# Second product of the expert network in 512 columns with two results added, later first counts, and pass A behind the first placement

## The chip, the cores and the metric

The kernel runs on one core of a Trainium2 chip. The metric is device time in microseconds (us) of one execution; the median of three runs of the kernel before is 1425.91 us.

## The reference

A Fourier filter along the sequence feeds a mixture of experts with eight experts, each with room for an eighth of the 19968 tokens:

```python
X = np.fft.rfft(x, axis=1)                      # x: 8 x 2496 x 256
y = np.fft.irfft(X * (filt_r + 1j * filt_i)[None], n=2496, axis=1)
tok = y.reshape(19968, 256)
logits = tok @ w_gate                           # 8 experts
# greedy: all (token, expert) pairs by falling logit; a pair is taken if the
# token is still free and the expert has fewer than 2496 tokens
for e in range(8):
    h = np.maximum(tok[mask_e] @ w1[e], 0.0)    # 256 -> 1024
    out[mask_e] = h @ w2[e]                     # 1024 -> 256
```

## The kernel before

The kernel has two stages that overlap a little: the Fourier filter as matmuls (class `Fft`, up to some 400 us), and the experts (class `Ffn`) one after the other. Routing (class `Route`) is done in eight phases. A phase finds the next expert to be full, with its members; it runs beside the network of the expert before it.

**The expert network.** An expert's 2496 tokens are five groups g: four of 512 and one of 448. A group's tokens are gathered, turned (L844) and split into a high and a low part of fp32r, whose sum is the fp32 value. `first` does the first product: for each of eight slices f of the hidden size, six matmuls of 512 columns into a PSUM tile `pz` (L864), then ScalarE's Relu writes the high part of the result and VectorE the low part, both in `hl` (L891, L893; in the last group L896, in two pieces). The second product runs over blocks t of 128 tokens (four in a group, the last one of the fifth group a half block of 64): in each step f, the stationary operand is a 128 x 128 piece of `hl` and the moving one 256 columns of the second weight. Three terms are summed: high times high (`w2h`), high times low (`w2l`), low times high, each one matmul of 256 columns into the PSUM tile `py` (L930). `py` has two buffers of tag "b". After 24 matmuls ScalarE copies `py` to `y` (L940) and a scatter on the GpSimd queue writes the rows out (L941). The half block puts high and low parts side by side as 128 columns of weights, in 16 matmuls, and adds the two halves of its result (L937, L938). The trace shows names of the first weight's tiles for some of the second's: `py<-w1h` in its rows is the product with `w2h`, and `pz<-xo,w0h` that with `w1h`.

**Weights.** `split` makes high and low tiles of the next expert's weights out of the loaded ones, eight parts of 512 columns an expert, ScalarE the high part and VectorE the low one (L823, L824).

**Routing beside it.** A phase from the second on begins with passes over the logits on VectorE: the maximum M (L644), two passes over `tmp` (L646, L648), the reduction to `ar` (L650), and pass A (L654), which marks for each token its best free expert. Eleven rounds of counts follow (`counts`): a comparison pass Gm on VectorE (L559), then eleven or thirteen short matmuls over Gm and A into a PSUM tile `rt` of tag "a" (two buffers; L567), three small VectorE passes (L575 to L577), and one matmul (L580) whose result sets the next threshold. The first count of a phase has three thresholds (nj = 3), the later ones seven or nine. When a phase has its members, `places` turns them to lists of rows for the gathers and the scatters, in five chunks, each with matmuls into `rt` (L777), VectorE passes (L778, L782) and ScalarE passes (L781). `s.last` is the VectorE instruction that ends the list of the first chunk (L787, L789).

**What sets the order.** TensorE's instructions are issued in the order in which the code is written. `Pump` sets where the routing's instructions go among the network's matmuls: each `yield` of the network gives the planner the time of the matmuls just issued, and each step of the routing gives a kind and a size, from which `lag` makes the time that must pass until the next step is issued. For a count, 'G' stands between the comparison pass and its matmuls, 'X' between the small passes and the matmul of L580. `ORD` says how many first products of the next group stand ahead of each block: one, none, none, one. The other engines' order is made by the framework's scheduler out of its own timeline; `issue_after` keeps an instruction behind another in it.

Of the kernel before, what the change touches and what calls it, by code (L numbers as in the profile page):

```python
# [7 lines left out]
F32, F32R = mybir.dt.float32, mybir.dt.float32r  # L8
# [7 lines left out]
G = 22  # L16
S = B * G
# [449 lines left out]
class Route:  # L467
# [169 lines left out]
    def phase(s, ph):  # L637
# [4 lines left out]
        if 0 < ph < 7:  # L642
            with s.tc.issue_after(s.last):
                nc.vector.tensor_reduce(s.M, s.lg, axis=AX.X, op=OP.max)  # L644
            yield 'd', 5.5
            nc.vector.tensor_tensor(s.tmp, s.lg, s.M.unsqueeze(2).to_broadcast([117, S, 8]), op=OP.is_equal)  # L646
            yield 'd', 1.5
            nc.vector.tensor_tensor(s.tmp, s.tmp, s.val[:117].unsqueeze(1).to_broadcast([117, S, 8]), op=OP.mult)  # L648
            yield 'd', 1.5
            nc.vector.tensor_reduce(s.ar, s.tmp, axis=AX.X, op=OP.max)  # L650
            nc.vector.scalar_tensor_tensor(s.ar, s.asg, 0.0, s.ar, op0=OP.is_equal, op1=OP.mult)
            yield 'd', 1.8
            n = s.n = 8 - ph
            nc.vector.tensor_tensor(s.A[:, :S*n].rearrange("p (s e) -> p s e", e=n), s.ar.unsqueeze(2).to_broadcast([117, S, n]),  # L654
                                    s.desc[:117, :n].unsqueeze(1).to_broadcast([117, S, n]), op=OP.is_equal)
            s.room()
            yield 'd', 1.5
        if ph < 7:
# [139 lines left out]
class Ffn:  # L798
# [9 lines left out]
    def weights(s, e, widx):  # L808
        nc = s.nc
        raw = [s.ww.tile([128, 2048], F32, name=f"wr{k}", bufs=1) for k in range(2)]  # L810
        off = bass.IndirectOffsetOnAxis(ap=widx[:, :1], axis=0)
        hl = [[s.ww.tile([128, 2048], F32R, name=f"w{k}{h}", bufs=2) for h in 'hl'] for k in range(2)]
        s.wt[e] = (raw, hl)
        s.load = lambda k: nc.gpsimd.indirect_dma_start(out=raw[k], out_offset=None, in_=(s.w1, s.w2)[k], in_offset=off).ins

    def split(s, e, part):

        nc = s.nc
        raw, hl = s.wt[e]
        k, h = divmod(part, 4)  # L820
        o = 512 * (h if k else 2 * (h % 2) + h // 2)
        src, hi, lo = (t[:, o:o+512] for t in (raw[k], *hl[k]))
        nc.scalar.copy(hi, src)  # L823
        nc.vector.tensor_tensor(lo, src, hi.bitcast(F32), op=OP.subtract)  # L824

# [24 lines left out]
    def run(s, e, pump, hook):  # L850
# [1 line left out]
        nc = s.nc  # L852
        ids = pump.out[e]
        out_rows = s.out
        _, ((w1h, w1l), (w2h, w2l)) = s.wt[e]
        hs = {}

        def products(p, f, g, a, b):
# [53 lines left out]
        for g in range(5):  # L912
            n = min(512, CAP - 512*g)
            yield from firsts(g, 8)
            if g == 4:
                hook('last')
            if g == 0:
                hook('w2')
            for t in range(4):
                if g < 4:  # L920
                    yield from firsts(g + 1, ORD[t])
                w = min(128, n - 128*t)
                p = s.ps.tile([128, D], F32, name="py", tag="b", bufs=2)
                half = w == 64
                hi, lo, both = slice(128*t, 128*t+w), slice(512+128*t, 512+128*t+w), slice(384, 512)
                terms = ((both, w2h), (hi, w2l)) if half else ((hi, w2h), (hi, w2l), (lo, w2h))
                m = 0
                for f in range(8):
                    for a, b in terms:
                        nc.tensor.matmul(p[:a.stop-a.start], hs[g][f][:, a], b[:, 256*f:256*f+256],  # L930
                                         start=m == 0, stop=m == 8 * len(terms) - 1, skip_group_check=half)
                        m += 1
                    if f in ((3,) if half else (1, 3, 5)):
                        yield 0.65
                y = s.wp.tile([128, D], F32, name="y", bufs=4)
                if half:
                    nc.scalar.copy(y[:w], p[w:])  # L937
                    nc.vector.tensor_tensor(y[:w], p[:w], y[:w], op=OP.add)  # L938
                else:
                    s.lasta = nc.scalar.copy(y, p).ins  # L940
                st = nc.gpsimd.indirect_dma_start(  # L941
                    out=out_rows, out_offset=bass.IndirectOffsetOnAxis(ap=ids[1][:w, 4*g+t:4*g+t+1], axis=0),
                    in_=y[:w], in_offset=None)
                for o in s.scat:
                    s.tc.declare_no_dep(st.ins, o.ins, reason="each token has one place")
                s.scat.append(st)
                if t in (1, 2) and g == 4:
                    hook(t)
                yield 0.65
# [147 lines left out]
class Pump:  # L1097
# [3 lines left out]
    def __init__(s, R):  # L1101
# [1 line left out]
        s.main, s.due, s.held = R.phase(0), 0.0, False  # L1103
        s.side = []
        s.on_w, s.kind = None, ''
        s.lag = dict(d=lambda t: t, G=lambda n: LAGS[s.ph][0] + 0.17 * n, X=lambda n: LAGS[s.ph][1], m=lambda t: 1.0 + 1.2*t, w=lambda t: t,
                     o=lambda t: t, p=lambda t: t, g=lambda t: 3.0)

    def step_main(s):
        if s.held:  # L1110
# [71 lines left out]
```

## Time and profile before

| | before |
|---|---|
| median of three runs | 1425.91 us (1425.71 to 1428.44) |
| the profiled execution | 1423.78 us, span 1422.0 us |
| TensorE matmul / weight loads | 97% / 86% of the span |
| VectorE / ScalarE / GpSimd | 63% / 47% / 35% |
| instructions of TensorE | 10412 matmuls, as many weight loads |
| mean granted clock of TensorE | 0.991 of full speed |

The rows are read so: "out<-in" are the program's names of the tiles, then partitions x elements, then how many; "idle before" is the time an engine stood before these instructions, and behind the arrow stands what ended it. Ends of matmuls are modelled, so that the pace of TensorE is read from one start to the next. A line of a stretch gives its start and end, its length, and the busy time of TensorE's matmuls, its weight loads, VectorE, ScalarE and GpSimd in it, with the number of instructions.

### The profile page before, as it was taken

How to read it: one execution, taken by the hardware profiler on the slowest of the kernel's cores; microseconds unless marked ns; L12 is line 12 of the kernel's file. 1: busy time of each engine (PE TensorE's matmuls, PEld its weight loads, DVE VectorE, ACT ScalarE, POOL GpSimd, SP SyncE). 2: the span in 40 equal slices, each digit the busy share in tenths (PEclk: the TensorE clock that was granted, in tenths of full speed). 3: DMA queues.
4: the chain of work that ended last, by engine and by line, in shares of the span. 5: the costliest groups of instructions: out<-in, count | busy, mean ns of one | idle time of the engine just before them, and what ended most of it. 6: DMA issues, size and time to landing. Idle time of an engine off the chain costs nothing.

```text
span 1422.0 us, 27350 instructions
## 1 busy us (share of the span) xinstructions
PE 1385.4 (97%) x10412; PEld 1216.9 (86%) x10412; DVE 893.8 (63%) x2554; ACT 672.0 (47%) x1632; POOL 503.6 (35%) x562
## 2 busy tenths in 40 slices
PE   9999999999989999999999999999999999999997
PEld 8998898976467898988789889888898998898987
DVE  5577676775667777568667876866867634423231
ACT  6766676645544254236335534523623635423231
POOL 3344343443034135324322733343334324333312
PEclk9999999999989999999999999999999999999999
DMA  9665664539961022112112212112111311111100
GB/s 375 250 228 182 197 217 132 165 106 297 367 224 58 16 97 66 36 53 78 50 33 83 67 43 89 46 48 99 46 44 50 136 52 55 47 39 50 40 19 28
DMA packets 57846, 153.12 MB, mean 108 GB/s; under 512 B 11023, under 2 KB 31519, under 8 KB 54131
## 3 DMA queue, kind: packets, MB, share of 16 engines
q0 software_dynamic: 22720, 72.67, 15.6%
q1 hardware_dynamic: 29132, 73.39, 14.9%
q10 hardware_dynamic: 5863, 5.31, 1.1%
q8 instruction: 82, 1.34, 0.4%
q14 instruction: 49, 0.40, 0.1%
HBM read 88.32 MB, written 63.06 MB: 106 GB/s over the span
## 4 chain that ended last, share of the span: by engine, by line
PE 42%; issue 6%; DVE 4%; POOL 1%; ACT 1%; DMA 0%; POOLq 0%; ACTq 0%; another core or an unknown queue 0%; DVEq 0%
PE py L930 20%; PE pz L864 19%; PE ptr L844 2%; POOL out L941 1%; PE rt L567 1%; PE rt L777 1%; DVE hl L896 1%; DVE w1l L824 0%; DVE hl L893 0%; DVE M L644 0%; DVE tmp L646 0%; ACT junka L781 0%; DVE tmp L648 0%; ACT hl L891 0%; DVE Gm L559 0%
## 5 line engine op out<-in xcount | busy, mean ns | idle before, releaser
L930 PE MATMUL py<-w1h,hl 128*128 128x256 f32 x2496 | 481.6, 286 | 0.8 <-DVE hl L896 0.8
L930 PEld LDWEIGHTS py<-w1h,hl 128*128 128x128 f32 x2496 | 400.9, 191 | 3.6 <-DVE hl L896 1.2
L930 PE MATMUL py<-w1l,hl 128*128 128x256 f32 (+1 forms) x1280 | 358.1, 282 | 0.0
L941 POOL DMA_INDIRECT out<-y,oid x160 | 169.2, 1058 | 501.1 <-ACT y L940 452.6
L891 ACT ACTIVATE hl<-pz 128x512 fp32r<-128x512 f32 (+1 forms) x320 | 187.7, 588 | 229.4 <-PE pz L864 186.6
L864 PE MATMUL pz<-xo,w0h 128*128 128x512 f32 (+2 forms) x646 | 265.8, 411 | 2.7 <-DVE hl L893 1.2
L893 DVE SCALAR_TENSOR_TENSOR hl<-pz,hl 128x512 fp32r<-128x512 f32 x256 | 175.4, 687 | 139.3 <-ACT hl L891 136.5
L864 PE MATMUL pz<-xo,w0l 128*128 128x512 f32 (+2 forms) x646 | 251.5, 389 | 0.0
L864 PE MATMUL pz<-z,w0h 128*128 128x512 f32 (+2 forms) x646 | 251.1, 389 | 0.3
L930 PEld LDWEIGHTS py<-w1l,hl 128*128 128x128 f32 (+1 forms) x1280 | 239.8, 187 | 2.1
L830 POOL DMA_INDIRECT xg<-xs,xid x160 | 172.4, 1077 | 145.9 <-issue 54.8
L940 ACT COPY y<-py 128x256 f32<-128x256 f32 x152 | 56.6, 372 | 304.6 <-PE py L930 265.8
L864 PEld LDWEIGHTS pz<-xo,w0l 128*128 128x128 f32 x646 | 122.6, 190 | 24.1
L864 PEld LDWEIGHTS pz<-xo,w0h 128*128 128x128 f32 x646 | 123.8, 192 | 22.0 <-DVE hl L893 2.4
L864 PEld LDWEIGHTS pz<-z,w0h 128*128 128x128 f32 x646 | 123.5, 191 | 17.0 <-DVE z L848 0.9
L219 ACT COPY Y<-p 64x240 f32<-64x240 f32 (+1 forms) x302 | 115.3, 382 | 29.0 <-PE p L213 21.9
L237 POOL TENSOR_TENSOR P<-P 128x256 f32<-128x256 f32 x80 | 58.7, 734 | 162.8 <-DVE P L235 162.6
L559 DVE TENSOR_TENSOR Gm<-M,thr 117x1232 bf16<-117x1232 f32 (+2 forms) x80 | 104.4, 1315 | 0.2
L213 PE MATMUL p<-cS,xr 117*128 117x120 f32 x688 | 93.9, 276 | 2.8 <-ACT Y L219 1.5
L213 PEld LDWEIGHTS p<-cS,xr 117*128 117x128 f32 x688 | 85.4, 191 | 6.8 <-ACT Y L219 4.3
L229 PE MATMUL p<-cW,Y 128*128 128x128 f32 x640 | 88.4, 276 | 0.6 <-DVE Q L236 0.6
L229 PEld LDWEIGHTS p<-cW,Y 128*128 128x128 f32 x640 | 80.0, 191 | 5.7 <-issue 3.9
(229 smaller groups left out, 2013.2 us busy)
## 6 DMA issues: line engine op xcount, KB each, us to landing
zd<-zt SPq DMA_DIRECT2D x60, 256.0 KB
xs<-xo SPq DMA_DIRECT2D x17, 600.0 KB
xr<-x SPq DMA_DIRECT2D x6, 1536.0 KB
z<-zd SPq DMA_DIRECT2D x14, 600.0 KB
xr<-x SPq DMA_DIRECT2D x6, 1216.0 KB
xs<-Y SPq DMA_DIRECT2D x10, 600.0 KB
zd<-zt ACTq DMA_DIRECT2D x20, 256.0 KB
z<-zd POOLq DMA_DIRECT2D x7, 600.0 KB
```

The costliest lines, as they stand in the source:

```text
L213: s.lastmm = nc.tensor.matmul(p[:, q-q0, :120], xv[:, q-24*h], s.cS1, start=True, stop=True).ins
L219: c = (nc.vector.tensor_copy if (t == 5 if b else cp) else nc.scalar.copy)(dst, src)
L229: nc.tensor.matmul(p[:, k], s.Y1[b][:, 4*g+k, dh*128:dh*128+128], s.cW[:, 4*g+k], start=True, stop=True)
L237: nc.gpsimd.tensor_tensor(P[:, :, :64], P[:, :, :64], P[:, :, 64:], op=OP.subtract)
L559: nc.vector.tensor_tensor(Gm[:, s0:s1, :m], s.M[:, s0:s1].unsqueeze(2).to_broadcast([117, s1 - s0, m]), thr[:117].unsqueeze(1).to_broadcas ...
L830: s.lastg = s.nc.gpsimd.indirect_dma_start(out=xg[:n], out_offset=None, in_=s.xs, in_offset=bass.IndirectOffsetOnAxis(ap=ids[0][:n, t:t+1] ...
L864: nc.tensor.matmul(p[:, a:b], w[:, sl], x[:, k, a:b], start=m == 0, stop=m == 5, skip_group_check=True)
L891: s.lasta = s.R.relu = nc.scalar.activation(h[:, :n], p[:, :n], AF.Relu).ins
L893: s.R.low = nc.vector.scalar_tensor_tensor(l[:, :n], p[:, :n], 0.0, h[:, :n].bitcast(F32), op0=OP.max, op1=OP.subtract).ins
L930: nc.tensor.matmul(p[:a.stop-a.start], hs[g][f][:, a], b[:, 256*f:256*f+256], start=m == 0, stop=m == 8 * len(terms) - 1, skip_group_check ...
L940: s.lasta = nc.scalar.copy(y, p).ins
L941: st = nc.gpsimd.indirect_dma_start(out=out_rows, out_offset=bass.IndirectOffsetOnAxis(ap=ids[1][:w, 4*g+t:4*g+t+1], axis=0), in_=y[:w], i ...
```

## The change

It has three parts.

The second product. High and low part of the second weight lie in one tile `w2`, for each step f 256 columns of the high part and then 256 of the low one. A full block's step f has two matmuls now: the high part of `hl` against all 512 columns, into both halves of a `py` tile of [128, 2, 256], and the low part of `hl` against the 256 columns of the high part of the weight, into its first half. ScalarE copies the second half to `y`, and a new VectorE instruction adds the first half to it. The half block is as before, in the first half of the tile.

The later first counts. In the phases with `ph > 1` the first count (n == 3) gets 2.5 more in 'G' and 0.8 more in 'X'.

The moved pass. Pass A gets `issue_after(s.last)`.

```diff
@@ phase
-            nc.vector.tensor_tensor(s.A[:, :S*n].rearrange("p (s e) -> p s e", e=n), s.ar.unsqueeze(2).to_broadcast([117, S, n]),
-                                    s.desc[:117, :n].unsqueeze(1).to_broadcast([117, S, n]), op=OP.is_equal)
+            with s.tc.issue_after(s.last):
+                nc.vector.tensor_tensor(s.A[:, :S*n].rearrange("p (s e) -> p s e", e=n), s.ar.unsqueeze(2).to_broadcast([117, S, n]),
+                                        s.desc[:117, :n].unsqueeze(1).to_broadcast([117, S, n]), op=OP.is_equal)
@@ weights
-        hl = [[s.ww.tile([128, 2048], F32R, name=f"w{k}{h}", bufs=2) for h in 'hl'] for k in range(2)]
+        w2 = s.ww.tile([128, 8, 2, D], F32R, name="w2", bufs=2)
+        hl = [[s.ww.tile([128, 2048], F32R, name=f"w1{h}", bufs=2) for h in 'hl'], w2]
@@ split
-        src, hi, lo = (t[:, o:o+512] for t in (raw[k], *hl[k]))
+        src = raw[k][:, o:o+512]
+        if k:
+            hi, lo = (hl[1][:, 2*h:2*h+2, j] for j in range(2))
+            src = src.rearrange("p (f d) -> p f d", d=D)
+        else:
+            hi, lo = (t[:, o:o+512] for t in hl[0])
@@ run
-                p = s.ps.tile([128, D], F32, name="py", tag="b", bufs=2)
+                p = s.ps.tile([128, 2, D], F32, name="py", tag="b", bufs=2)
-                terms = ((both, w2h), (hi, w2l)) if half else ((hi, w2h), (hi, w2l), (lo, w2h))
-                    for a, b in terms:
-                        nc.tensor.matmul(p[:a.stop-a.start], hs[g][f][:, a], b[:, 256*f:256*f+256],
-                                         start=m == 0, stop=m == 8 * len(terms) - 1, skip_group_check=half)
+                    if half:
+                        nc.tensor.matmul(p[:, 0], hs[g][f][:, both], w2[:, f, 0], start=f == 0, stop=f == 7, skip_group_check=True)
+                        nc.tensor.matmul(p[:w, 0], hs[g][f][:, hi], w2[:, f, 1], start=False, stop=f == 7, skip_group_check=True)
+                    else:
+                        nc.tensor.matmul(p, hs[g][f][:, hi], w2[:, f], start=f == 0, stop=f == 7, skip_group_check=True)
+                        nc.tensor.matmul(p[:, 0], hs[g][f][:, lo], w2[:, f, 0], start=False, stop=f == 7, skip_group_check=True)
-                    s.lasta = nc.scalar.copy(y, p).ins
+                    s.lasta = nc.scalar.copy(y, p[:, 1]).ins
+                    nc.vector.tensor_tensor(y, p[:, 0], y, op=OP.add)
@@ Pump
-        s.lag = dict(d=lambda t: t, G=lambda n: LAGS[s.ph][0] + 0.17 * n, X=lambda n: LAGS[s.ph][1], m=lambda t: 1.0 + 1.2*t, w=lambda t: t,
+        s.lag = dict(d=lambda t: t, G=lambda n: LAGS[s.ph][0] + 0.17 * n + (2.5 if s.opens(n) else 0), X=lambda n: LAGS[s.ph][1] + (0.8 if s.opens(n) else 0), m=lambda t: 1.0 + 1.2*t, w=lambda t: t,
...
+    def opens(s, n):
+        return n == 3 and s.ph > 1
```

TensorE, end of the second expert, before: the end of a full block, a placement chunk (GE), and the first count (Gm) of the phase whose count has five experts.

```order
L930 MATMUL py<-w1l,hl 128x256
L930 MATMUL py<-w1h,hl 128x256 x2
L930 MATMUL py<-w1l,hl 128x256
L930 MATMUL py<-w1h,hl 128x256
L777 LDWEIGHTS GE
L777 MATMUL rt<-dt,GE 128x180
L777 LDWEIGHTS GE
L777 MATMUL rt<-dt,GE 128x180
L567 LDWEIGHTS Gm
L567 MATMUL rt<-A,Gm 48x80
```

The same full block and chunk in the changed kernel (line numbers are up to eight higher there; `w_6441` is `w2`):

```order
L939 MATMUL py<-w_6441,hl 128x256
L938 MATMUL py<-w_6441,hl 128x512
L939 MATMUL py<-w_6441,hl 128x256
L851 MATMUL ptr<-id,xg 128x128 x4
L778 LDWEIGHTS GE
L778 MATMUL rt<-dt,GE 128x180
L778 LDWEIGHTS GE
L778 MATMUL rt<-dt,GE 128x180
L935 MATMUL py<-w_6441,hl 128x256
L936 MATMUL py<-w_6441,hl 64x256
```

And the first count of that phase there, behind the sixteen matmuls of the half block that began above:

```order
L935 MATMUL py<-w_6441,hl 128x256
L936 MATMUL py<-w_6441,hl 64x256
L871 MATMUL pz<-xo,w1h 128x512
L871 MATMUL pz<-z,w1h 128x512
L871 MATMUL pz<-xo,w1l 128x512
L567 LDWEIGHTS Gm
L567 MATMUL rt<-A,Gm 48x80
```

The steps of the block have become pairs, and the count has moved from directly behind the chunk to behind the whole half block and three matmuls of the next expert.

VectorE at the same place, before: from the last step of `ar` to just behind pass A, with the last low halves (L896) of the group.

```order
L651 SCALAR_TENSOR_TENSOR ar<-asg,ar 117x176
L896 SCALAR_TENSOR_TENSOR hl<-pz,hl 128x384
L896 SCALAR_TENSOR_TENSOR hl<-pz,hl 128x64
L896 SCALAR_TENSOR_TENSOR hl<-pz,hl 128x384
L824 TENSOR_TENSOR w1l<-wr_8191,w1h 128x512
L792 TENSOR_REDUCE t1b<-t_8231 128x4
L782 TENSOR_SCALAR ex<-rt 128x4
L786 TENSOR_SCALAR js<-js 128x4
L654 TENSOR_TENSOR A<-ar,row 117x880
L778 TENSOR_TENSOR loc<-sidx,rt 128x2
```

The same in the changed kernel:

```order
L948 TENSOR_TENSOR y<-py,y 128x256
L651 SCALAR_TENSOR_TENSOR ar<-asg,ar 117x176
L793 TENSOR_REDUCE t1b<-t_8038 128x4
L783 TENSOR_SCALAR ex<-rt 128x4
L787 TENSOR_SCALAR js<-js 128x4
L655 TENSOR_TENSOR A<-ar,row 117x880
L795 SCALAR_TENSOR_TENSOR oid<-t1b,t_8160 128x4
L788 SCALAR_TENSOR_TENSOR xid<-ex,js 128x4
L791 TENSOR_TENSOR t_8038<-js,row 128x28
L794 TENSOR_TENSOR t_8245<-js,ex 128x4
L948 TENSOR_TENSOR y<-py,y 128x256
```

The low halves stand ahead of the last step of `ar` now, and adds of the second product (L948) stand before and behind pass A.

## Rows read from the trace of the kernel before

**Rows 1.** The page, its first lines: busy us, share of span, instructions.
```profile
span 1422.0 us, 27350 instructions
...
PE 1385.4 (97%) x10412; PEld 1216.9 (86%) x10412; DVE 893.8 (63%) x2554; ACT 672.0 (47%) x1632; POOL 503.6 (35%) x562
```

**Rows 2.** Busy us of each engine by stretch, then granted clock, DMA share, GB/s.
```profile
414.00:1110.00 696.00, 683.20 (x4997) 604.29 (x4998) 500.87 (x1630) 296.38 (x723) 257.97 (x235) 0.99 0.19 62
1110.00:1414.00 304.00, 303.03 (x2000) 275.38 (x2000) 111.35 (x304) 115.45 (x272) 91.30 (x95) 1.00 0.14 47
```

**Rows 3.** Timeline of TensorE, a calm place: start, us, instruction.
```profile
1263.52 0.39 PE L864 MATMUL pz<-z,w0h 128*128 128x512 f32 x1
...
1267.47 0.37 PE L864 MATMUL pz<-xo,w0h 128*128 128x448 f32 x1
...
1268.93 0.40 PE L930 MATMUL py<-w1h,hl 128*128 128x256 f32 x2
...
1275.36 0.40 PE L930 MATMUL py<-w1h,hl 128*128 128x256 f32 x2
```

**Rows 4.** Chain of waits in order of time, 1240 to 1300: start, us, pieces.
```profile
1245.37 8.56 PE py L930 x72
...
1263.26 5.60 PE pz L864 x24
```

**Rows 5.** Groups of instructions by line and form: busy us, mean ns; idle before.
```profile
L930 PE MATMUL py<-w1l,hl 128*128 128x256 f32 x1216 | 342.7, 282 | 0.0
...
L893 DVE SCALAR_TENSOR_TENSOR hl<-pz,hl 128x512 fp32r<-128x512 f32 x256 | 175.4, 687 | 139.3 <-ACT hl L891 136.5 <-issue 1.2
...
L941 POOL DMA_INDIRECT out<-y,oid x160 | 169.2, 1058 | 501.1 <-ACT y L940 452.6 <-issue 13.6 <-DVE GE L770 12.1
...
L940 ACT COPY y<-py 128x256 f32<-128x256 f32 x152 | 56.6, 372 | 304.6 <-PE py L930 265.8 <-PE rt L580 14.5 <-PE ptr L844 7.8
...
L559 DVE TENSOR_TENSOR Gm<-M,thr 117x1232 bf16<-117x1232 f32 x54 | 77.8, 1440 | 0.1
...
L938 DVE TENSOR_TENSOR y<-py,y 64x256 f32<-64x256 f32 x8 | 3.3, 416 | 16.6 <-ACT y L937 11.3 <-issue 5.3
```

**Rows 6.** Waits of TensorE from 414 us on: us in total, times, longest.
```profile
PE rt L580 <- DVE X L577: 4.3, 3, 2.4
...
PE ptr L844 <- DVE hl L893: 0.2, 1, 0.2
```

**Rows 7.** Timeline of TensorE, first counts of three later phases.
```profile
673.20 0.58 PE L567 MATMUL rt<-A,Gm 117*48 117x80 bf16 x11 [1.56 <-PE rt L777]
...
909.31 0.46 PE L567 MATMUL rt<-A,Gm 117*48 117x48 bf16 x11 [0.96 <-remote]
...
1022.47 0.45 PE L567 MATMUL rt<-A,Gm 117*48 117x32 bf16 x11 [0.39 <-DVE ex L782]
```

**Rows 8.** The five crowded stretches, columns as in rows 2.
```profile
523.00:543.00 20.00, 19.96 (x138) 18.42 (x138) 20.00 (x71) 11.80 (x37) 14.34 (x11) 1.00 0.23 72
650.00:671.00 21.00, 20.16 (x139) 18.49 (x139) 20.71 (x73) 12.66 (x39) 12.59 (x11) 1.00 0.19 58
777.00:798.00 21.00, 20.12 (x147) 18.34 (x146) 20.73 (x80) 13.13 (x41) 16.46 (x12) 1.00 0.22 69
885.00:906.00 21.00, 20.32 (x130) 17.06 (x129) 20.66 (x62) 12.41 (x37) 10.27 (x10) 1.00 0.17 50
1005.00:1022.00 17.00, 17.00 (x116) 14.57 (x114) 16.80 (x54) 11.41 (x38) 11.70 (x11) 1.00 0.25 79
```

**Rows 9.** Timelines of TensorE, VectorE and ScalarE in the second of them.
```profile
665.34 0.40 PE L930 MATMUL py<-w1h,hl 128*128 128x256 f32 x2
...
666.78 0.40 PE L930 MATMUL py<-w1h,hl 128*128 128x256 f32 x2
...
668.14 0.50 PE L930 MATMUL py<-w1h,hl 128*128 128x256 f32 x2 [0.84 <-DVE hl L896]
...
669.45 1.06 DVE L654 TENSOR_TENSOR A<-ar,row 117x880 bf16<-117x880 f32 x1
...
670.67 0.41 ACT L781 ACTIVATE junka<-rt,loc 128x176 bf16<-128x176 f32 x1 [1.15 <-DVE A L654]
```

**Rows 10.** Timeline of a half block: matmuls, then two of its weight loads.
```profile
1299.31 0.28 PE L930 MATMUL py<-w1h,hl 128*128 128x256 f32 x1
...
1300.01 0.39 PE L864 MATMUL pz<-xo,w0h 128*128 128x512 f32 x1
...
1299.43 0.19 PEld L930 LDWEIGHTS py<-w1h,hl 128*128 128x128 f32 x1
1299.54 0.14 PEld L930 LDWEIGHTS py<-w1l,hl 128*64 128x64 f32 x1
```

More of the change, by code (lines that the diff above doesn't have):

```diff
@@ L854, in run @@
         out_rows = s.out
-        _, ((w1h, w1l), (w2h, w2l)) = s.wt[e]
+        _, ((w1h, w1l), w2) = s.wt[e]
         hs = {}
@@ L922, in run @@
                 w = min(128, n - 128*t)
-                p = s.ps.tile([128, D], F32, name="py", tag="b", bufs=2)
+                p = s.ps.tile([128, 2, D], F32, name="py", tag="b", bufs=2)
                 half = w == 64
                 hi, lo, both = slice(128*t, 128*t+w), slice(512+128*t, 512+128*t+w), slice(384, 512)
-                terms = ((both, w2h), (hi, w2l)) if half else ((hi, w2h), (hi, w2l), (lo, w2h))
-                m = 0
                 for f in range(8):
-                    for a, b in terms:
-                        nc.tensor.matmul(p[:a.stop-a.start], hs[g][f][:, a], b[:, 256*f:256*f+256],
-                                         start=m == 0, stop=m == 8 * len(terms) - 1, skip_group_check=half)
-                        m += 1
+                    if half:
[4 more added lines that the diff above has]
+                        nc.tensor.matmul(p[:, 0], hs[g][f][:, lo], w2[:, f, 0], start=False, stop=f == 7, skip_group_check=True)
                     if f in ((3,) if half else (1, 3, 5)):
@@ L936, in run @@
                 if half:
-                    nc.scalar.copy(y[:w], p[w:])
-                    nc.vector.tensor_tensor(y[:w], p[:w], y[:w], op=OP.add)
-                else:
-                    s.lasta = nc.scalar.copy(y, p).ins
+                    nc.scalar.copy(y[:w], p[w:, 0])
+                    nc.vector.tensor_tensor(y[:w], p[:w, 0], y[:w], op=OP.add)
+                else:
+                    s.lasta = nc.scalar.copy(y, p[:, 1]).ins
+                    nc.vector.tensor_tensor(y, p[:, 0], y, op=OP.add)
                 st = nc.gpsimd.indirect_dma_start(
```

## The prediction

> **What bounds the kernel now.** I read the page first. TensorE's share of busy time is 97% [rows 1], and the table by stretch says where the other engines matter: from 414 us on the expert network runs, VectorE is 72% busy until the last routing is done near 1110 us, and 37% busy after that [rows 2]. Of the 1000 us of that stage the list of TensorE's own waits names thirteen kinds, from 4.3 us down to 0.2, and 13.7 us together [rows 6]. So the stage is as long as the matmuls take at their pace, plus a few waits. The granted clock is full (1.00, the 2.4 GHz level) in the calm half [rows 2], so the pace is not lost to the clock there.
>
> The pace itself I take from a calm place in TensorE's timeline, from start to start, since ends are modelled. Seventeen 512-column matmuls go from 1263.52 to 1267.47, which is 232.4 ns each. Fifty-four 256-column matmuls of the second product go from 1268.93 to 1275.36, which is 119.1 ns each [rows 3]. Two halves cost 238.2, one whole 232.4: the part that doesn't depend on columns is some 5.8 ns.
>
> **Term 1, the wider matmul.** For every one of the 152 full blocks of 128 tokens, each of the eight steps f had three 256-column matmuls and now has one of 512 and one of 256. Columns stay the same (768 a step). By the two paces a step goes from 3 x 119.1 = 357.3 to 232.4 + 119.1 = 351.5, so 5.8 ns are saved in 1216 steps (the count of the L930 rows with the low half [rows 5]): 7.0 us. Bounds: the chain of waits has 72 of the small ones in 8.56 us and 24 of the large in 5.60 [rows 4], which makes 4.5 ns a step and 5.5 us. In a stretch under load the small ones stand 120.0 ns apart (twelve from 665.34 to 666.78 [rows 9]), which makes 7.6 ns and 9.2 us. I take 7.0, from the longest undisturbed piece. The half blocks (64 tokens) keep their sixteen matmuls, so nothing there. No wait hides this term: it is on TensorE, which is the path.
>
> The Trainium skill (TensorE: Matmul & The Clock Gate, section Back-to-back issue gap) gives a full-clock matmul N/2.4 plus 2.5 ns; by it a step would save 2.5 ns and the term would be 3.0 us, as an estimate from that page. The rows differ (119.1 and 232.4 against 109.2 and 215.8), and I go by the rows.
>
> **Term 2, the added VectorE pass.** Each of the 152 blocks gets one more instruction: the copy on ScalarE stays (372 ns), and VectorE adds the other half from PSUM. Its nearest row is the add of the half blocks, 64 x 256 at 416 ns [rows 5], with the same columns. 152 x 0.416 is 63 us of VectorE. After 1110 us it falls into an engine that is 37% busy and hides whole. Before that, the average (72%) hides it too, but not the mean decides: there are five stretches of 17 to 21 us in which VectorE is busy 98.9 of 100 us [rows 8], one for each routing phase from the third on, when the passes over the logits, the next expert's weight split and the last group's low halves (L896) come together. What is added there makes everything behind it late.
>
> How late TensorE becomes is told by its busy time in these stretches. In the first and the last (from 523 and from 1005 us) it lost next to nothing; in the middle three it lost 0.8, 0.9 and 0.7 us [rows 8], and in one of them the wait is a matmul at 668.14 that waited 0.84 us for L896 [rows 9]. So the first and last still have cover, and the middle three have none. In the order of the changed kernel one, two and four adds stand, in these three, between the maximum pass and the last low half of the group: seven adds, 7 x 0.416 = 2.9 us. If the other two stretches (three and four adds) had no cover either, it is 14 x 0.416 = 5.8; if the scheduler's places are all harmless, 0. I take +2.9.
>
> The first product's results, queued behind the added instruction on VectorE, are waited for by the second product one block later; the scatter on the GpSimd queue waits for the add as well, some 0.45 us longer, but there it already sat idle 452.6 us for this very copy [rows 5] and the gathers behind it are issued a group ahead. I cost that at nothing; without that cover it would be 0.45 us a block. The weight split writes the same 512 elements in two runs of 256, at no cost.
>
> **Term 3, the later first counts and the moved pass.** The first count of a phase is eleven short matmuls that need a PSUM buffer of tag "a", which the placement work holds, and pass A. In the trace these counts made TensorE wait 1.56 us at 673.20, 0.96 at 909.31 and 0.39 at 1022.47 [rows 7], 2.9 us in all, and none in the other two phases it changes. The 1.56 is read backwards so: pass A (1.06 us at 669.45) held VectorE, so the ScalarE pass at 670.67 began 1.15 us late, and with it the buffer came free late [rows 9]. In the changed order the same count stands behind a half block and three 512-column matmuls, so 16 x 0.117 + 3 x 0.232 = 2.6 us of TensorE's work later. VectorE in turn gets there later by the adds ahead of pass A, at most three, 1.25 us. Cover left: 1.3 us. Recovered: 1.3 of the 1.56, and 0.96 and 0.39 whole: 2.6 us. Bounds: 0 (the next buffer or chain is late instead) and 2.9. The extra constraint on pass A costs nothing where it stood behind that instruction already, as it did. The later counts push routing back by about 2.5 us in each of five phases, some 12 us at the end; the placement of an expert is still ahead of the group that asks for it, so nothing waits.
>
> **Sum.** -7.0 + 2.9 - 2.6 = -6.7 us. The profiled execution took 1423.78 us with a span of 1422.0, which makes 1417.1; the median of the three runs is 2.1 us above it, and from that I get 1425.91 - 6.7 = 1419.2 us.
>
> **Rivals.** *VectorE takes it back (no change).* The pair saves only the lower 5.5, all five crowded stretches pay (+5.8), and the waits at the counts move to the next instruction (0): 1426.2 us. For it: VectorE is full there. Against it: only three of the five lost time at all. The variant that the pair brings nothing (a 256-column matmul behind a wide one at 125 ns) ends in the same place, 1426. Together 0.22.
>
> *Slower: the second product's buffers come free late.* Two PSUM buffers serve these blocks, and block t+2 needs the one of block t. Behind the first block of a group two more follow with no first product between, so there are 8 x 0.3515 = 2.81 us from its end to the next use, of which the copy and the add take 0.79. Two us remain for queues. An add that comes behind a comparison pass (1.44 us) and two low halves (0.69 each) [rows 5] is 0.8 us too late, and TensorE stands. There are 25 such first blocks in the five experts during which routing runs; all of them late is +20 us, 1439. It decides the sign from twelve late blocks on (12 x 0.8 = 9.6 against 6.7 + 2.85). For it: in the changed order several of these adds do stand directly behind a comparison pass. Against it: seldom two low halves more. I give 0.14, around 1431.
>
> *Much faster: the weight loads set the pace.* Loads are 86% of the span [rows 1]; were the 119.1 ns the pace of a load, a step with two loads could shrink to its columns. At the full clock 768 columns are 320 ns, so 37 ns less in 1216 steps: 45 us, 1375 to 1380. Against it: in the half blocks every other load has 64 columns and takes 0.14 us against 0.19, and the matmuls still go six in 0.70 us, 116.7 ns each [rows 10]. I give 0.04. The Trainium skill (Perfetto Trace Analysis, section Identifying the Most-Contended Engine) wants TensorE's headroom read from the share of its weight loads, by which this rival would be the case; the half blocks speak against it.
>
> **How the numbers follow.** The forecast has 0.60, with 1414 to 1423 as its own range (largest gain 9.2 + 2.9, smallest just past the threshold). The no-change case has 0.22, slower 0.14, much faster 0.04. A difference of 0.2% (2.85 us) is about what a measurement of this kernel can tell from none, so faster 0.64, same 0.22, slower 0.14. The range takes in the forecast and the no-change case and leaves out the two outer rivals: 1413.5 to 1428.
>
> **What would show it.** Term 1: in calm stretches a wide and a narrow matmul of the second product together 351 ns from start to start of the next pair; 358 means it brought nothing, 325 the last rival. Term 2: in the crowded stretches VectorE still full, TensorE's loss there up by about 3 us in sum, and no steady wait of the third block of a group on the add; a total of such waits over 9 us is the slower rival. Term 3: no wait over 0.3 us of the first counts of the later phases. I am wrong if the added pass shows up as waits outside the crowded stretches, or if the waits that go from the first counts turn up at the counts behind them. The longest single wait, 2.4 us before an L580 [rows 6], stands in the first expert, where only the added passes reach; I leave it as it is, and its going or doubling would move the time by as much.

## The result: 1% slower where it was timed, no change on two other chips

The changed kernel took 1441.59 us (median of 8 runs, 1436.8 to 1446.96) against 1426.24 us for the kernel before on the same chip (8 runs, 1425.44 to 1431.5): ratio 1.0096, interval 1.0078 to 1.0114. The forecast was 1419.2 us, faster; the range ended at 1428. On two other chips, 7 and 13, the same two kernels later measured 0.9999 and 1.0002 (the table in the next section).

| | before | after |
|---|---|---|
| profiled execution | 1423.78 us, span 1422.0 | 1440.06 us, span 1438.3 |
| matmuls / weight loads, share of span | 97% / 86% | 96% / 80% |
| VectorE | 63% | 66% |
| matmuls | 10412 | 9196 |

First the page of the changed kernel, which answers to [rows 1]: busy time, share and instructions of each engine.

```profile
span 1438.3 us, 25186 instructions
...
PE 1385.1 (96%) x9196; PEld 1149.7 (80%) x9196; DVE 949.9 (66%) x2706; ACT 672.0 (47%) x1632; POOL 498.4 (35%) x562
```

Its table by stretch has the columns of [rows 2]; the expert network ends some 17 us later than before.

```profile
414.00:1110.00 696.00, 670.01 (x4089) 545.81 (x4090) 521.16 (x1664) 288.93 (x708) 249.02 (x232) 0.99 0.18 58
1110.00:1432.00 322.00, 317.45 (x1699) 267.48 (x1697) 148.94 (x427) 124.70 (x291) 97.92 (x100) 0.99 0.16 52
```

Until 1110 us TensorE is idle for 26.0 us (the length less its busy time), against 12.8 in [rows 2]; after that for 4.6 against 1.0. The pace itself is better, as a calm place of its timeline shows (answering to [rows 3]):

```profile
1285.86 0.40 PE L938 MATMUL py<-w,hl 128*128 128x512 f32 x1
...
1293.96 0.40 PE L938 MATMUL py<-w,hl 128*128 128x512 f32 x1
```

These are the first and the last of 24 wide matmuls with a narrow one between each two: 8.10 us for 23 steps, 352.2 ns a step against 357.3 before. So the new matmuls are a little faster, as they were meant to be, and TensorE stands still more. The list of its waits from 416 us on answers to [rows 6] (total us, times, longest; the six largest of eighteen kinds):

```profile
PE rt L580 <- DVE X L577: 7.7, 5, 5.8
PE rt L778 <- DVE pf L711: 2.4, 1, 2.4
PE pz L871 <- DVE hl L900: 2.2, 4, 0.9
PE pz L871 <- ACT xo L854: 2.1, 2, 1.9
PE py L939 <- DVE hl L903: 2.0, 4, 1.3
PE py L938 <- DVE y L948: 1.6, 1, 1.6
```

Only the last of these names the added add (L948), and once. The groups that answer to [rows 5] show the add as it was sized, 422 ns, and the scatter that now waits for it:

```profile
L948 DVE TENSOR_TENSOR y<-py,y 128x256 f32<-128x256 f32 x152 | 64.1, 422 | 119.4 <-ACT y L947 113.7 <-issue 4.8
...
L949 POOL DMA_INDIRECT out<-y,oid x159 | 166.4, 1046 | 510.1 <-DVE y L948 329.1 <-DVE di L619 30.7 <-DVE loc L779 30.3
```

### The profile page after: what moved, and what is told of

It reads as the page before. It is cut to its first block, busy times and chain, and to the rows that moved or that the text cites. A ratio compares the mean times of both kernels' runs of the same rounds, so it can differ in the third digit from the quotient of the medians.

```text
span 1438.3 us, 25186 instructions
## 1 busy us (share of the span) xinstructions
PE 1385.1 (96%) x9196; PEld 1149.7 (80%) x9196; DVE 949.9 (66%) x2706; ACT 672.0 (47%) x1632; POOL 498.4 (35%) x562
## 4 chain that ended last, share of the span: by engine, by line
PE 75%; issue 8%; DVE 7%; ACT 4%; DMA 3%; POOL 2%; another core or an unknown queue 0%; POOLq 0%; ACTq 0%; DVEq 0%
PE pz L871 24%; PE py L938 15%; PE py L939 7%; PE p L213 5%; PE p L229 5%; PE pa L284 4%; PE pv L395 3%; PE pa L248 2%; DMA xs<-Y 2%; PE ptr L851 2%; PE rt L567 2%; PE pv L257 2%; POOL out L949 1%; DVE hl L903 1%; ACT lg L752 1%
## 5 line engine op out<-in xcount | busy, mean ns | idle before, releaser
L938 PE MATMUL py<-w,hl 128*128 128x512 f32 x1216 | 444.9, 404 | 1.7 <-DVE y L948 1.6
L939 PE MATMUL py<-w,hl 128*128 128x256 f32 x1216 | 341.7, 281 | 2.0 <-DVE hl L903 2.0
L871 PE MATMUL pz<-xo,w1h 128*128 128x512 f32 (+2 forms) x646 | 265.8, 412 | 8.8 <-DVE hl L900 2.2
L938 PEld LDWEIGHTS py<-w,hl 128*128 128x128 f32 x1216 | 228.9, 188 | 51.1 <-DVE y L948 2.3
L871 PE MATMUL pz<-z,w1h 128*128 128x512 f32 (+2 forms) x646 | 252.3, 391 | 1.8 <-DVE z L855 1.2
L871 PE MATMUL pz<-xo,w1l 128*128 128x512 f32 (+2 forms) x646 | 251.8, 390 | 0.0
L939 PEld LDWEIGHTS py<-w,hl 128*128 128x128 f32 x1216 | 229.6, 189 | 5.2 <-DVE hl L903 3.5
L871 PEld LDWEIGHTS pz<-xo,w1h 128*128 128x128 f32 x646 | 123.4, 191 | 33.2 <-DVE hl L900 3.2
L948 DVE TENSOR_TENSOR y<-py,y 128x256 f32<-128x256 f32 x152 | 64.1, 422 | 119.4 <-ACT y L947 113.7
L871 PEld LDWEIGHTS pz<-xo,w1l 128*128 128x128 f32 x646 | 123.0, 190 | 24.8 <-issue 0.6
L871 PEld LDWEIGHTS pz<-z,w1h 128*128 128x128 f32 x646 | 123.7, 191 | 19.6 <-DVE z L855 2.9
```

Of the source, the lines that this page charges most:

```text
L871: nc.tensor.matmul(p[:, a:b], w[:, sl], x[:, k, a:b], start=m == 0, stop=m == 5, skip_group_check=True)
L938: nc.tensor.matmul(p, hs[g][f][:, hi], w2[:, f], start=f == 0, stop=f == 7, skip_group_check=True)
L939: nc.tensor.matmul(p[:, 0], hs[g][f][:, lo], w2[:, f, 0], start=False, stop=f == 7, skip_group_check=True)
L948: nc.vector.tensor_tensor(y, p[:, 0], y, op=OP.add)
```

## The experiments

The runs fell on several chips, and this turned out to matter. The chip on which the change was timed is called the timing chip here; it may be one of the others. Ratios are to the kernel before on the same chip at the same time, with their 95% interval; differences in us below are these ratios times the kernel before.

| chip, kernel before | kernel: ratio (interval) |
|---|---|
| timing of the change, 1426.2 us | change 1.0096 (1.0078 to 1.0114) |
| chip 1, 1412.3 us | product alone 1.0009 (0.9998 to 1.0020); later counts alone 0.9986 (0.9978 to 0.9995); 8 y buffers 0.9995 (0.9983 to 1.0007); pass added to the old kernel 1.0040 (1.0027 to 1.0053) |
| chip 7, 1411.6 us | change 0.9999 (0.9989 to 1.0009); product and counts 1.0007 (0.9995 to 1.0019); product and moved pass 1.0012 (1.0003 to 1.0022); change without add 0.9946 (0.9930 to 0.9962) |
| chip 2, 1411.0 us | add on GpSimd 1.0037 (1.0024 to 1.0051) |
| chip 13, 1411.1 us | change 1.0002 (0.9991 to 1.0013); product alone 1.0007 (0.9995 to 1.0018); later counts alone 0.9996 (0.9987 to 1.0006); change without add 0.9958 (0.9944 to 0.9973) |
| chip 3, 1428.4 us | mixed 1.0099 (1.0072 to 1.0125); inverse 1.0134 (1.0115 to 1.0154) |
| chip 2 again, 1412.2 us | later counts alone 0.9996 (0.9982 to 1.0009); product alone 1.0014 (1.0002 to 1.0026) |

**The parts, one by one.** The trace of the changed kernel suggested a chain: y has four buffers, a buffer is free when its scatter has landed, the scatter waits for the add. The rival was that the moved counts had fallen into worse places. Product alone:

```diff
-  G=... + (2.5 if s.opens(n) else 0), X=... + (0.8 if s.opens(n) else 0)
+  G=..., X=...
-            with s.tc.issue_after(s.last):
-                nc.vector.tensor_tensor(s.A...)
+            nc.vector.tensor_tensor(s.A...)
```

> The changed kernel without its second half: the wider second product with its added VectorE pass stays, the first counts of phases 2 and later and the pass that makes A stand again where they stood before. Theory L (the added pass: it makes each row block's y go out later, and what stands behind the copy, the add and the scatter on ScalarE, VectorE and GpSimd waits): the loss is all here, 1438 to 1444 us, the stalls of TensorE after 410 us near the 42 us of the changed kernel against 23 us before. Theory M (the moved counts and the moved pass fell into worse places): the product alone gains what was forecast for it or half of it, 1419 to 1427 us.

The later counts and the moved pass in the kernel before (the same lines the other way round):

> The kernel before with only the later first counts (+2.5 and +0.8) and the moved pass of the other two tries; the second product stays in 256 columns with no added pass. Theory L: as forecast for that part or no change, 1422 to 1427 us. Theory M: the loss is here, 1434 to 1442 us.

The changed kernel with more buffers:

```diff
-                y = s.wp.tile([128, D], F32, name="y", bufs=4)
+                y = s.wp.tile([128, D], F32, name="y", bufs=8)
```

> The changed kernel with 8 buffers for y in place of 4, nothing else. Theory L1 (a y buffer is free only when its scatter has landed; the scatter now waits for the add and for its turn in the GpSimd queue, so ScalarE stands at the copy into y, with the relus and placements behind it): the loss goes, 1420 to 1428 us, and the ScalarE waits of up to 5.0 us ahead of the copies into y at ends of experts fall under 1 us. Theory L2 (VectorE's 64 us of added work by themselves, wherever they stand): within 3 us of the changed kernel, 1438 to 1444 us.

The added pass in the old kernel:

```diff
                     s.lasta = nc.scalar.copy(y, p).ins
+                    nc.vector.tensor_tensor(y, p, y, op=OP.max)
```

> The kernel before with one more VectorE pass over every full row block between the copy and the scatter: the maximum of the product in PSUM and its copy in y, which is the copy again, so nothing in the result changes; 152 passes of the size and the operands of the add. The matmuls are those of before. Theory L (either form): slower than before by what the changed kernel lost plus the pace that it had gained, 1440 to 1450 us. Theory M: the pass hides, 1426 to 1430 us.

The expected times were written for a kernel before of 1426 us; on chip 1 it took 1412.3, so the ratios count. They make +1.3, -2.0, -0.7 and +5.6 us. None of the four showed the lost 15 us. The added pass alone was the one clear cost, and the later counts alone a small gain. Whether the y buffers had brought them back could only be said with the changed kernel on such a chip.

**The change on another chip, and its two halves.**

> The changed kernel itself, word for word, beside the runs of the kernel before on the same chip, since the kernel before took 1412.3 us where the four parts ran and 1426.2 us where the change was timed. Theory I (the two halves cost nothing one by one but 1% together, and 8 buffers of y give it back): ratio 1.006 to 1.011 here too. Theory C (the loss belongs to the chip on which the change was timed, whose transfers land later): where the kernel before takes about 1412 us the ratio is 0.998 to 1.003; where it takes about 1426 us it is 1.006 to 1.011.

With pass A where it stood (without issue_after), and with the counts where they stood (without the 2.5 and 0.8):

> The wider second product with its added pass and the later first counts, but the pass that makes A where it stood before. Theory I, counts: ratio 1.006 to 1.011. Theory I, pass: ratio 0.999 to 1.002. Theory C: within 0.002 of the product alone wherever it runs.

> The wider second product with its added pass and the moved pass that makes A, but the first counts where they stood before. Theory I, pass: ratio 1.006 to 1.011. Theory I, counts: ratio 0.999 to 1.002. Theory C: within 0.002 of the product alone wherever it runs.

The change took what the kernel before took, and so, within 0.13%, did both halves with the product. So the loss goes with the chip, or with something else that differed between these runs and the first; chip 2, which had two sets of runs, gave the kernel before 1411.0 and 1412.2 us. The halves don't harm each other here. The y buffers fall as a cause here: the trace with 8 buffers (chip 1) and that of the changed kernel (chip 7) hold the same TensorE instructions in the same order, and from the first matmul of the expert network to the last their starts drift apart by 0.05 us, and at no place by more than 0.12.

**What the add costs.** The change without the line `nc.vector.tensor_tensor(y, p[:, 0], y, op=OP.add)`:

> The changed kernel without the VectorE add over full row blocks: y is the copy of the second half of the product alone, so the first half is left out of the result. It prices the add where the matmuls are wide. If the pace gained is 3 to 4 us and the add costs what the maximum in the narrow kernel did (4.8 us on that chip), this is 5 to 9 us under the changed kernel, ratio to the kernel before 0.994 to 0.997 where the changed kernel is at 1.001, 1.000 to 1.004 where it is at 1.010.

This kernel leaves half of each result out. It is 7.5 us under the change on chip 7, and 6.2 us on chip 13, each with some 2.6 us either way by the intervals. The TensorE instructions being the same, the two traces of chip 7 can be subtracted start by start: 5.6 us. Nearly all of it comes up in eight or nine pieces of 8 us, and of these all but 0.4 us lie in the five crowded stretches. The table by stretch shows it, columns as in [rows 8] (the fourth stretch, then the sum of all five). The changed kernel:

```profile
884.00:906.00 22.00, 20.36 (x113) 16.62 (x111) 20.02 (x65) 13.58 (x42) 10.40 (x9) 1.00 0.17 53
...
sum 102.00, PE 94.72 PEld 77.72 DVE 89.55 ACT 62.85 POOL 52.15; mean PE 18.94 PEld 15.54 DVE 17.91 ACT 12.57 POOL 10.43
```

Without the add:

```profile
884.00:906.00 22.00, 21.82 (x121) 18.31 (x120) 20.95 (x72) 14.95 (x48) 12.09 (x11) 1.00 0.18 54
...
sum 102.00, PE 98.80 PEld 82.35 DVE 88.27 ACT 67.01 POOL 55.58; mean PE 19.76 PEld 16.47 DVE 17.65 ACT 13.40 POOL 11.12
```

TensorE stands 7.3 us of 102 with the adds, 3.2 without. These windows are cut by the clock and don't fit the crowding exactly: in the changed kernel VectorE works with no idle over 0.3 us from 517 to 542, 649 to 668, 772 to 792, 888 to 911 and 1003 to 1027 us, and 18 of the 152 adds stand there.

**The add on GpSimd.**

```diff
-                y = s.wp.tile([128, D], F32, name="y", bufs=4)
+                y2 = s.wp.tile([128, 2, D], F32, name="y", bufs=4)
+                y = y2[:, 0]
-                    s.lasta = nc.scalar.copy(y, p[:, 1]).ins
-                    nc.vector.tensor_tensor(y, p[:, 0], y, op=OP.add)
+                    s.lasta = nc.scalar.copy(y2, p).ins
+                    nc.gpsimd.tensor_tensor(y, y, y2[:, 1], op=OP.add)
```

> The changed kernel with the add of full row blocks on GpSimd: ScalarE copies both halves of the product (512 columns) into a y buffer of twice the size, GpSimd adds one half onto the other in front of its own scatter. If VectorE's share is what the add costs (7 us on the chip where the other eight ran), most of that comes back: ratio to the kernel before 0.995 to 0.998 there. If the later scatter and the y buffers are what it costs, nothing comes back, since the add on GpSimd is longer: 1.000 to 1.006.

Worse than the kernel before, by 5.2 us. One add takes 0.81 us there and ScalarE's copy 0.59 instead of 0.37; which of these, or which queue, carries the loss was not tried.

**The kernel before on another chip.**

> The kernel before, for its trace on this chip, to be laid beside its trace on the chip where the change was timed, instruction by instruction. On a chip where it takes about 1412 us Theory C expects the pace of the matmuls to be the same within 0.5 us over the whole stretch, and all of the 10 to 14 us in single jumps: places where ScalarE or VectorE start over 0.5 us later than the TensorE instruction they wait for was recorded as done. If the pace itself differs instead, the other chip is simply slower and Theory C falls.

Both kernels now had traces from two chips, word for word the same program. From the first matmul of the expert network to its last, the changed kernel on the timing chip and on chip 7:

```profile
415.47 0.38 PE L871 MATMUL pz<-xo,w1h 128*128 128x256 f32 x1 [0.95 <-ACT X L635]
...
1430.93 0.28 PE L936 MATMUL py<-w,hl 128*64 128x256 f32 x1
...
416.04 0.38 PE L871 MATMUL pz<-xo,w1h 128*128 128x256 f32 x1 [0.77 <-ACT xo L854]
...
1402.19 0.28 PE L936 MATMUL py<-w,hl 128*64 128x256 f32 x1
```

The kernel before, on the timing chip and on chip 2:

```profile
414.31 0.58 PE L864 MATMUL pz<-xo,w0h 128*128 128x256 f32 x1 [0.67 <-ACT xo L847]
...
1414.58 0.28 PE L930 MATMUL py<-w1l,hl 128*64 128x256 f32 x1
...
415.51 0.39 PE L864 MATMUL pz<-xo,w0h 128*128 128x256 f32 x1 [0.67 <-ACT xo L847]
...
1402.10 0.28 PE L930 MATMUL py<-w1l,hl 128*64 128x256 f32 x1
```

So over the network the change falls 29.3 us behind, the kernel before 13.7 us. Taken matmul by matmul, 19.0 of the 29.3 us are longer waits of TensorE (over 0.15 us), 6.1 lie in stretches at the lower clock, and 4.3 are small steps; of the 13.7 us it is 8.5, 2.7 and 2.4. The drift grows in jumps. The largest one, 5.9 us, is at a second count (L580) in the second expert. First the timing chip, in order of time:

```profile
683.01 0.57 PE L567 MATMUL rt<-A,Gm 117*48 117x80 bf16 x11
...
686.55 0.33 PE L778 MATMUL rt<-dt,GE 117*128 117x180 f16 x2
...
687.55 0.37 ACT L944 COPY y<-py 64x256 f32<-64x256 f32 x1 [5.04 <-PE rt L778]
...
691.88 0.23 DVE L575 TENSOR_TENSOR t<-rt,row 48x80 f32<-48x80 f32 x1 [3.51 <-remote]
...
691.93 1.08 ACT L898 ACTIVATE hl<-pz 128x512 fp32r<-128x512 f32 x2 [4.01 <-remote]
...
692.64 0.20 PE L580 MATMUL rt<-X,ones 128*128 128x15 f16 x1 [5.75 <-DVE X L577]
```

The same place on chip 7:

```profile
674.04 0.37 ACT L944 COPY y<-py 64x256 f32<-64x256 f32 x1
...
674.64 0.58 PE L567 MATMUL rt<-A,Gm 117*48 117x80 bf16 x11
...
675.31 0.22 DVE L575 TENSOR_TENSOR t<-rt,row 48x80 f32<-48x80 f32 x1
...
676.15 0.60 ACT L898 ACTIVATE hl<-pz 128x512 fp32r<-128x512 f32 x1 [1.73 <-PE pz L871]
...
678.22 0.17 PE L580 MATMUL rt<-X,ones 128*128 128x15 f16 x1
```

L575 waits in the program for nothing but the last of the eleven count matmuls L567 (and for its place behind L945). On chip 7 it starts 0.10 us after their recorded end, on the timing chip 8.29 us after, while TensorE's own rows go on at their pace. The copy L944 waits for the half block's last matmul; the wait for its y buffer was over at 682.02. So VectorE and ScalarE see TensorE's work late, and TensorE then stands for what they make; such a start is called a late release below. The records of TensorE's semaphore, by which it releases the others, say the same: five instructions that update it end at 680.67 to 686.88 us, and no update is on record from 681.01 to 687.53 and from there to 691.86. On chip 7 each of the five is followed by an update within 0.02 us. Of the waits of ScalarE and VectorE for TensorE, some 50 begin over 1 us later after the recorded end than on chip 7, in ten episodes or so, most at ends of experts; in the kernel before it is just under 30, none over 3.3 us later (how many depends on how a wait is matched to its matmul).

A trace of this kind of chip is also less complete. In the four traces of it (both kernels on the timing chip, and the two runs on chip 3 below) 40 to 49 of the 1500 to 1600 updates of TensorE's semaphore are missing, and 145 to 167 of VectorE's, all in the expert network; the other sixteen traces lack at most two of TensorE's. So here "<-remote" can also mean that the update that ended a wait isn't on record. Behind the longest late release the clock falls too (columns as in [rows 2], granted clock third from the end):

```profile
691.00:697.00 6.00, 4.36 (x17) 3.41 (x17) 4.79 (x17) 2.94 (x8) 1.68 (x2) 0.59 0.05 13
```

While TensorE stood from 686.9 to 692.6 the granted clock fell to its lower level, 1.2 GHz, and part of this stretch ran at it. In all, the clock is at this level for 13.7 us of the changed kernel's network behind 430 us, each time next to a wait of TensorE of 1.9 us or more; on chip 7 it isn't there at all.

**Once more, on chip 13.**

> The changed kernel once more. Theory C: ratio to the kernel before 0.998 to 1.002 where that takes about 1412 us, 1.006 to 1.011 where it takes about 1426 us, and in the second case its trace shows waiters on ScalarE and VectorE that start 1 to 8 us after the TensorE instruction they wait for, in the same episodes at the ends of experts.

> The product with its added pass, alone, once more. About 1.001 where the kernel before takes 1412 us. Where it takes 1426 us: 1.005 to 1.011 if the late releases come with the added VectorE pass, 0.999 to 1.003 if they come with the moved counts.

> The later first counts and the moved pass, alone, once more. About 0.9986 where the kernel before takes 1412 us. Where it takes 1426 us: 0.996 to 1.001 if the late releases come with the added VectorE pass, 1.005 to 1.011 if they come with the moved counts.

> The changed kernel without the add of full row blocks (the first half of the product is left out of the result), once more. About 0.995 where the kernel before takes 1412 us. Where it takes 1426 us: 0.993 to 0.998 if the late releases come with the added VectorE pass, 1.002 to 1.007 if they come with the wider matmuls or the moved counts.

Chip 13 gave the ratios of chips 1 and 7 again, within 0.12%.

**The add in the crowded stretches alone, and everywhere else alone.** The mixed kernel has the old three matmuls where `wide` is false, in the crowded stretches, and the new two elsewhere; the inverse kernel has `in` for `not in`:

```diff
+CROWD = {0: range(15, 19), 1: range(15, 19), 2: range(15, 19), 3: range(11, 15), 4: range(7, 12)}
+                wide = 4*g + t not in CROWD.get(e, ())
+                    elif not wide:
+                        nc.tensor.matmul(p[:, 0], hs[g][f][:, hi], w2[:, f, 0], ...)
+                        nc.tensor.matmul(p[:, 0], hs[g][f][:, hi], w2[:, f, 1], ...)
+                        nc.tensor.matmul(p[:, 0], hs[g][f][:, lo], w2[:, f, 0], ...)
+                elif not wide:
+                    s.lasta = nc.scalar.copy(y, p[:, 0]).ins
```

> The changed kernel with the old 256-column product, and so without the add, in the 21 row blocks of the five stretches in which VectorE is full (blocks 15 to 18 of experts 0 to 2, 11 to 14 of expert 3, 7 to 11 of expert 4, counted from 0 in each expert); the other 131 full blocks keep the wide product and the add. If the add costs only where VectorE is full: nearly all of its 5.6 us comes back for some 0.7 us of pace, ratio to the kernel before 0.995 to 0.998. If it costs by its number, wherever it stands (152 adds, 21 left out): a seventh of it comes back, ratio 0.999 to 1.001.

> The other way round: the wide product and the add in those 21 row blocks only, the old product in the other 131. If the add costs only where VectorE is full: as slow as the whole change or slower, since the pace is gone and the cost is not, ratio to the kernel before 1.001 to 1.005. If it costs by its number: near the later first counts alone, 0.998 to 1.001.

These two fell on a chip where the kernel before takes 1428 us, so they answer another question as well. By their medians they are 4.7 us apart (1442.33 and 1447.02), the mixed one ahead, though it has 131 adds and the other 21; the intervals touch. So each lost about 1% to this chip on top, which neither expectation had. The fourth and the fifth crowded stretch (experts 3 and 4) are free of late releases in the change on the timing chip, and there the picture is plain. The inverse kernel has the one wait on an add that the change has (its lines are L943 and L955):

```profile
915.20 0.49 PE L943 MATMUL py<-w,hl 128*128 128x512 f32 x1 [1.60 <-DVE y L955]
```

On chip 7 the change has it too:

```profile
898.88 0.50 PE L938 MATMUL py<-w,hl 128*128 128x512 f32 x1 [1.64 <-DVE y L948]
```

The mixed kernel has none. Adding up, in these two stretches, what TensorE's starts stand apart over their pace (gaps over 0.15 us): 1.8 and 1.4 us in the change, 1.8 and 1.5 with the 21 adds, 0.3 and 0.9 with the 131, 0.3 and 0.9 with none. So here the adds in the crowded stretches carry the whole cost; for the other three stretches the traces of these two kernels can't say it, since late releases lie in them. In the fourth stretch nearly all of the cost is that one wait of 1.6 us, which is the slower rival's: a PSUM buffer held by a late add.

For the chip's own loss they say that it doesn't go by the number of wide blocks or of adds: 1.010 with 131, 1.013 with 21. What remains in common is the second half of the change, the new tiles (two halves in PSUM, w2 with high and low part interleaved), and the fact that any such change puts all engines' instructions in another order. The last two runs were to part the first two of these:

> The later first counts and the moved pass, alone, a third time. Where the kernel before takes about 1412 us: 0.998 to 1.001. Where it takes about 1427 us: with 131 wide blocks or with 21 the change was at 1.010 and 1.013 there, so the wide product and its adds are not what loses; if the moved counts are, this is at 1.008 to 1.014 too, and if it is the new tiles (two halves in PSUM, high and low part interleaved in w2), it is at 0.997 to 1.002.

> The wide product with its adds, alone, a third time. Where the kernel before takes about 1412 us: 0.999 to 1.002. Where it takes about 1427 us: 0.999 to 1.003 if the moved counts are what loses there, 1.006 to 1.012 if it is the new tiles.

They fell on chip 2, where they took 0.9996 and 1.0014, as on the other chips of its kind, and so this stays open.

## Why the prediction was wrong

**Term 1 held, at the lower end.** Forecast 7.0 us (5.5 to 9.2). The pace gives 5.1 ns in 1216 steps, 6.2 us; the change without its add against the later counts alone on chip 13 (0.9958 against 0.9996) gives 5.4 us, with some 2.4 us either way. The pair was to stand 351 ns apart and stands at 352.2. The formula that the Trainium skill (TensorE: Matmul & The Clock Gate, section Back-to-back issue gap) has for the gap of an isolated matmul would give 2.5 ns a step; the trace's 5.1 ns doesn't agree.

**Term 2 was mis-sized: 5.6 to 7.5 us in place of 2.9.** The place was right (VectorE full in five stretches, and the loss there). The step that failed is the count: seven adds in three stretches, and none in the first and the last, because TensorE had lost next to nothing there. On chip 7 all five lose, by the sums of gaps 1.2, 0.9, 0.6, 1.5 and 0.5 us, 4.7 in all. The first and the last, put at nothing, make 1.7 of it: a stretch in which TensorE just keeps up and VectorE is full has no cover. The middle three make 3.0, as forecast, but half of that is luck: it is the one wait of 1.6 us by the slower rival's mechanism, a PSUM buffer held by a late add, which the sum had at nothing and which occurs once in 25 first blocks. So the upper end, 5.8, was near for a reason that is only in part the stated one. The added pass alone in the old kernel cost about the same (1.0040; 5.9 us start by start, chip 1 against chip 2). That the scatter's delay costs nothing fits: 8 buffers changed nothing.

**Term 3 was read from waits that belong to a chip.** Forecast 2.6 us from the waits of 1.56, 0.96 and 0.39 us [rows 7]. Here is the kernel before at the first and the third of these places on chip 2; at the second the count waited for nothing.

```profile
666.97 0.57 PE L567 MATMUL rt<-A,Gm 117*48 117x80 bf16 x11 [0.32 <-DVE ex L782]
...
1012.10 0.45 PE L567 MATMUL rt<-A,Gm 117*48 117x32 bf16 x11 [0.39 <-DVE ex L782]
```

There are 0.7 us to recover, and the part alone measured -0.6, -0.6 and -2.0 us (only the last clear of zero). The reading of the 1.56 by way of pass A [rows 9] was a story: 1.24 us of it are drift against the other chip.

**The sum on chips 7 and 13** is thus about -5.5 + 6.5 - 1 = 0, the rival "VectorE takes it back", which had 0.22.

**What was not in the sum at all** is the result's own loss of 15 us. The step that failed is the first one of the prediction: that the stage is the matmuls' pace "plus a few waits", all of which but three at the counts I left as they were, with no reason to think that they would stay. On the timing chip the kernel before already ran 13.7 us behind itself on chip 2, 8.5 of it in waits, and I took its waits as the kernel's. The longest of them stood in the table: 2.4 us before an L580 [rows 6], of which I said only that its doubling would move the time. The row behind it, in the kernel before on the timing chip:

```profile
440.37 0.70 PE L567 MATMUL rt<-A,Gm 117*128 117x112 bf16 x11
...
444.09 0.28 DVE L575 TENSOR_TENSOR t<-rt,row 112x112 f32<-112x112 f32 x1 [3.36 <-remote]
```

The count was done at 441.07, and L575 started 3.02 us later, "<-remote": the profile names nothing that released it. On chip 2 the same instruction follows in 0.04 us. In the change the distance to the other chip grew by 15.6 us (29.3 less 13.7), which is the loss: 10.4 us of it in waits of TensorE, most behind late releases (its wait of 5.75 us above is the longest), 3.4 in stretches at 1.2 GHz, the rest in small steps. Why the late releases grow is not shown. It isn't the number of adds or of wide matmuls; whether it is the moved counts, the new tiles or merely another order of instructions was not settled, because the parts alone never ran on such a chip. Nor was it tried whether the recording of the trace takes part.

## What to carry to other kernels

Where a side engine is full for a stretch, instructions added there cost time, also if the engine behind it still kept up: here 18 adds of 0.42 us cost 4.7 us in five such stretches. Count all of them, not only those that already lose. To leave the change out in them took the cost away in the two stretches where it could be read; as a time it wasn't measured on a chip of the faster kind. A wait for an engine that was recorded as done long before may not belong to the kernel: lay it beside a trace from a second chip before a term is built on removing it, and before a 1% difference is put down to the code.

## What the runs showed of the hardware

The kernel before took 1411 to 1412 us on four chips and 1426 to 1428 us where the change was timed and on chip 3. Between chips 1 and 7 the expert network's TensorE starts agree to 0.05 us over 986 us (0.12 at most), so that whole traces can be subtracted instruction by instruction. A stretch at the lower clock breaks this: with the product alone, chip 13 falls 1.5 us behind chip 2 in one such stretch from 790.6 us, and the rest runs in step. On the slower kind, ScalarE and VectorE started up to 8.3 us after the recorded end of the TensorE instruction that they wait for (0.04 us is usual, the median of some 700 such waits), in episodes that lie at the same kind of place in each kernel, and semaphore updates are missing from the records there. In the episode above the semaphore's own update is late as well, so the waiting engines aren't alone in it; whether TensorE's recorded ends are too early can't be read from a trace. The time is lost either way.
